# Decode attention with a gated MLP on one core: probabilities written by ScalarE, one accumulator row block, and another order of the last weight loads

## The chip, the cores and the metric

One core of a Trainium2 chip runs the whole program. The metric is the device time of one execution in microseconds (us). The kernel before takes 348.27 us (median of 3 runs, 348.23 to 348.41).

## What is computed

One decode step for two batch rows: attention over a long cache, a small MLP, and a gate that mixes the two.

```python
# x: (2, 1, 512), K and V cache: (2, 32 heads, 4096, 128), all bf16
g = sigmoid((x * gate_w).sum(-1))
q = (x @ wq) as 32 heads of 128          # wq: 512 x 4096
p = softmax(q . k_cache / sqrt(128))     # per batch row and head, over 4096 keys
a = (p . v_cache) as 4096 values @ wo    # wo: 4096 x 512
b = relu(x @ w1) @ w2                    # w1: 512 x 1376, w2: 1376 x 512
out = g * a + (1 - g) * b                # (2, 1, 512)
```

K and V are 134 MB together; the four weight matrices add 11 MB. Every byte is read once.

## The kernel before

**Steps.** The work is cut into `NS` = 16 steps. Step `s` takes four heads (`T` = 4) of one batch row; `quad(s)` gives group `g` of eight heads, batch row `b` and half `i`, so a group is complete after four steps (`SPG` = 4), and there are `NG` = 4 groups. K and V of a step are 4 MB each, laid as 128 partitions: head t has partitions 32t to 32t+31, and each partition has 128 keys (`NC`) of 128 elements. K has two buffers (`kpool`), V two (`vpool`).

**One step.** VectorE multiplies K with the query in two halves (`mult`, L219, in place). TensorE sums blocks of the products with an identity matrix into PSUM (`red`, L225, 16 matmuls of 128x512 a half), and VectorE finishes the sum to one score per key (`scores`, L237). ScalarE takes the exponential and the row sums (`probs`, L243: one instruction of 128x128 into a tile `e`, sums into `partials`). VectorE spreads `e` into a zero-padded tile `PT_sb`, in which the four heads' probabilities stand in four columns beside each other (`expand`, L257, a multiply with a mask `tmask`). TensorE multiplies `PT_sb` with V (`pv`, L278, 32 matmuls of 32 weight columns each, in four column groups). Sums over the partitions of a head come from a small matmul (`sums_mm`, L263), their reciprocal times the gate from VectorE (`sums_inv`). ScalarE empties the result out of PSUM with that scale (`evac`, L289), TensorE picks out each head's own column (`comb`, L304), and every second step VectorE writes the finished head outputs into `OT_sb` (`unpack`, L318 and L322).

**Output.** The product with wo (`wo_mm`) and the MLP's second product (`mlp_o`) both add into one PSUM tile `a_ps`, which stays open for the whole kernel. `accumulate` (L326) makes each product as two matmuls of 256 columns, for the left and the right half of the output, in two separate column groups of the array, so `a_ps` is 34 partitions by 256 columns (rows 0 and 1 the left half, rows 32 and 33 the right). At the end one VectorE copy (L442) takes all 34 partitions to `res`, and two DMAs (L444), one issued by SP and one by ScalarE, write the two halves out.

**Order.** The order on each engine is the order in which the program issues it; no scheduler moves anything. All loads are issued by SP, so they form one queue over the 16 DMA engines. A load waits on SP until its buffer is free: K of step s+2 until `red` of step s has read the buffer, V of step s+1 until `pv` of step s-1 has. On TensorE a step runs `sums_mm(s-1)`, `comb(s-2)`, `red(s)`, `pv(s-1)`. On ScalarE it runs `probs(s)`, `evac(s-1)`.

**Loads of weights.** wq is loaded whole first and its 4 MB buffer is later taken by wo. wo of group 0 is loaded in step 2 and of group 1 in step 6. The other two groups, the last two MB of wo, and the whole of w2 follow the last V (L418 to L424), after V of the last step, which comes in three pieces (half, quarter, quarter). After the loop come the last step's `pv`, `evac`, `comb` and `unpack`, with the products of group 2 put around them, then group 3 and w2.

Of the kernel before, what the change touches and what calls it, by code (L numbers as in the profile page):

```python
# [13 lines left out]
T = 4  # L14
# [3 lines left out]
GH = 8  # L18
WH = 16
PT_SLOTS = 3  # L20
AG = 2


@with_exitstack
def kernel(
# [38 lines left out]
    DR = GH * Dh // P  # L64
    DA = Dh // DR
    CW = P // IG
    AR = CG * (AG - 1) + B
    inv_sqrt_dh = 1.0 / (float(Dh) ** 0.5)
    FF = Dff // P
    FREM = Dff - FF * P  # L70
# [102 lines left out]
    nc.vector.memset(heads, 0.0)  # L173
    for t in range(T):
        nc.vector.memset(heads[t * TP : (t + 1) * TP, t::T], 1.0)
    tmask = consts.tile([P, T], bf16, name="tmask")
    nc.vector.memset(tmask, 0.0)
    for t in range(T):
        nc.vector.memset(tmask[t * TP : (t + 1) * TP, t : t + 1], 1.0)
    PT_sb = consts.tile([P, PT_SLOTS, NQ, CG], bf16, name="PT_sb")  # L180
    nc.vector.memset(PT_sb, 0.0)
    umask = consts.tile([P, DA], fp32, name="umask")
# [3 lines left out]
    partials = consts.tile([P, NS], fp32, name="partials")  # L186
    OT_sb = consts.tile([P, NG, DR, B], bf16, name="OT_sb")
    w2_sb = consts.tile([P, FC, D], bf16, name="w2_sb")
    a_ps = apool.tile([AR, D // AG], fp32, name="a_ps")
    nc.vector.memset(a_ps, 0.0)  # L190
    g_sb = consts.tile([P, B], fp32, name="g_sb")
    omg = consts.tile([P, B], fp32, name="omg")
    hT = consts.tile([P, B, FC], bf16, name="hT")
# [15 lines left out]
            nc.scalar.copy(out=qb[:, b], in_=ps.rearrange("p (i d) -> p i d", d=Dh))  # L209
        qb_t[w] = qb  # L210

    red_t, sc_t, e_t, o_t, osb_t, rsg_t, comb_t = {}, {}, {}, {}, {}, {}, {}

    def mult(s, u):
        g, b, i = quad(s)
        w, gi = divmod(g * IG + i, IW)
        q = qb_t[w][:, b, gi, :].unsqueeze(1).to_broadcast([P, CU, Dh])
        kt = k_t[s][:, u * CU : (u + 1) * CU, :]
        nc.vector.tensor_tensor(out=kt, in0=kt, in1=q, op=ALU.mult)  # L219

    def red(s, u):
        prod = k_t[s][:, u * CU : (u + 1) * CU, :]
        ps = redp.tile([P, CU, RW], fp32, name="red")
        for j in range(Dh // RW):
            nc.tensor.matmul(  # L225
                ps,
                lhsT=ident,
                rhs=prod[:, :, j * RW : (j + 1) * RW],
                start=(j == 0),
                stop=(j == Dh // RW - 1),  # L230
            )
        red_t[s, u] = ps

    def scores(s, u):
        if u == 0:
            sc_t[s] = smalls.tile([P, NC], fp32, name="sc")
        nc.vector.reduce_sum(  # L237
            out=sc_t[s][:, u * CU : (u + 1) * CU], in_=red_t.pop((s, u)), axis=AX.X
        )

    def probs(s):
        e = smalls.tile([P, NC], bf16, name="e")
        nc.scalar.activation(  # L243
            out=e,
            in_=sc_t.pop(s),
            func=ACT.Exp,
            scale=inv_sqrt_dh,
            accum_out=partials[:, s : s + 1],
        )
        e_t[s] = e  # L250

    def expand(s):
        e = e_t.pop(s).rearrange("p (q j) -> p q j", j=JB).unsqueeze(3)
        m = tmask.unsqueeze(1).unsqueeze(1)
        out_ = PT_sb[:, s % PT_SLOTS, :, : JB * T].rearrange("p q (j t) -> p q j t", t=T)
        shape = [P, NQ, JB, T]
        nc.vector.tensor_tensor(  # L257
            out=out_, in0=e.to_broadcast(shape), in1=m.to_broadcast(shape), op=ALU.mult
        )

    def sums_mm(s):
        gs = gsp.tile([P, 1], fp32, name="gs")
        nc.tensor.matmul(gs, lhsT=heads, rhs=partials[:, s : s + 1], start=True, stop=True)  # L263
        rsg_t[s] = gs

    def sums_inv(s):
        rsg = smalls.tile([P, 1], fp32, name="rsg")
        nc.vector.reciprocal(out=rsg, in_=rsg_t[s])
        b = quad(s)[1]
        nc.vector.tensor_tensor(out=rsg, in0=rsg, in1=g_sb[:, b : b + 1], op=ALU.mult)  # L270
        rsg_t[s] = rsg

    def pv(s):
        vt = v_t.pop(s)
        o_ps = opool.tile([P, JB * Dh], fp32, name="o_ps")
        for q in range(NQ):
            k = q % NCG
            nc.tensor.matmul(  # L278
                o_ps[k * CG : (k + 1) * CG, :],
                lhsT=PT_sb[:, s % PT_SLOTS, q, :],  # L280
                rhs=vt[:, q * JB : (q + 1) * JB, :],
                start=(q < NCG),
                stop=(q >= NQ - NCG),
            )
        o_t[s] = o_ps

    def evac(s):
        osb = smalls.tile([P, JB, Dh], fp32, name="osb")
        nc.scalar.activation(  # L289
            out=osb,  # L290
            in_=o_t.pop(s).rearrange("m (j d) -> m j d", d=Dh),
            func=ACT.Copy,
            scale=rsg_t.pop(s),
        )
# [28 lines left out]

    def accumulate(lhsT, rhs, start, stop):
        for k in range(AG):
            nc.tensor.matmul(  # L326
                a_ps[k * CG : k * CG + B, :],
                lhsT=lhsT,
                rhs=rhs[:, k * (D // AG) : (k + 1) * (D // AG)],
                start=start,  # L330
                stop=stop,
            )

    def wo_mm(g, r0=0, r1=DR):
        for r in range(r0, r1):
            accumulate(OT_sb[:, g, r, :], wo_t[g][:, r, :], g == 0 and r == 0, False)

    def gate():
        gwT = transposed(gw_sb, 1, "gwT")
# [31 lines left out]
        if FREM:  # L371
            nc.vector.memset(hT[: P - FREM, :, FF:], 0.0)

    w2_view = B_w2[: FF * P].rearrange("(p f) j -> p f j", f=FF)

    def load_w2(f0, f1):
        nc.sync.dma_start(out=w2_sb[:, f0:f1, :], in_=w2_view[:, f0:f1, :])

    def load_w2_rest():
        nc.sync.dma_start(out=w2_sb[:, FF, :], in_=B_w2[Dff - P :, :])  # L380

    def mlp_o(f0, f1):
        for f in range(f0, f1):
            accumulate(hT[:, :, f], w2_sb[:, f, :], False, f == FC - 1)

    for w in range(NW):
        make_qb(w)
    for s in range(NS):
        if s >= 1:
            sums_mm(s - 1)  # L390
        if s >= 2:
            comb(s - 2)
        mult(s, 0)
        if s == 0:
            gate()
        if s >= 1:
            sums_inv(s - 1)
            expand(s - 1)
        if s >= 2:
            unpack(s - 2)  # L400
        red(s, 0)
        mult(s, 1)
        scores(s, 0)
        red(s, 1)
        scores(s, 1)
        probs(s)
        if s >= 1:
            pv(s - 1)
            evac(s - 1)
        if s % SPG == 1 and SPG < s < NS - SPG:  # L410
            wo_mm(s // SPG - 1)
        if s == 5:
            mlp_h()
        if s % SPG == 2 and s < NS - 2 * SPG:
            load_wo(s // SPG)
        load_k(s + 2)
        load_v(s + 1)
        if s + 1 == NS - 1:  # L418
            load_wo(NG - 2)
            load_wo(NG - 1)  # L420
            load_w2(0, 4)
            load_w2(4, 7)
            load_w2(7, FF)
            load_w2_rest()  # L424

    s = NS - 1
    expand(s)
    sums_mm(s)
    sums_inv(s)
    comb(s - 1)  # L430
    unpack(s - 1)
    pv(s)
    evac(s)
    wo_mm(NG - 2, 0, DR // 2)
    comb(s)
    unpack(s)
    wo_mm(NG - 2, DR // 2, DR)
    wo_mm(NG - 1)
    mlp_o(0, FC)

    res = consts.tile([AR, D // AG], bf16, name="res")
    nc.vector.tensor_copy(out=res, in_=a_ps)  # L442
    for k, queue in enumerate((nc.sync, nc.scalar)):
        queue.dma_start(  # L444
            out=out[:, 0, k * (D // AG) : (k + 1) * (D // AG)],
            in_=res[k * CG : k * CG + B, :],
        )


# [28 lines left out]
```

The softmax here doesn't subtract the row's maximum and nothing guards it: scores larger than these inputs give would overflow.

## Time and profile before

| What | Value |
| --- | --- |
| Median of 3 runs | 348.27 us (348.23 to 348.41) |
| The profiled execution's own time | 348.23 us |
| Its span in the profile | 346.5 us (1.73 us lie around it) |
| Read from HBM | 145.46 MB, 420 GB/s over the span |
| TensorE matmul busy | 214.3 us (62%) |
| VectorE busy | 184.1 us (53%) |
| ScalarE busy | 21.8 us (6%) |
| Mean granted TensorE clock | 0.813 of full speed |

The span runs from the first to the last recorded event of one execution. A row of ten digits or more in the profile shows a busy share in tenths over 40 equal slices of the span, here of 8.66 us each. A row of a group of instructions has the source line, the engine, the operation, the tile written and those read, the shapes and count, then the total busy time and the mean of one in nanoseconds, then the idle time just before them and what ended it. In a timeline, the columns are start in us, duration in us, engine, line, operation and count, and in brackets the idle time before with what ended it. Neighbours of one kind are merged there, and their duration is then that of the batch.

### The profile page before, as it was taken

Reading aid. Unit: us, or ns where it says so; the run is one execution under the profiler, and the core shown is the slowest. Engines: PE = TensorE matmul, PEld = TensorE weight load, DVE = VectorE, ACT = ScalarE, POOL = GpSimd, SP = SyncE. Lnnn points to the kernel's source line nnn. Section 1 sums busy time; section 2 is a strip of 40 time slices with the busy share of each in tenths; the row PEclk is TensorE's granted clock in tenths of the full one; section 3 lists DMA queues with packets and bytes.
Section 4 is the critical chain, followed back from the end, with each engine's and each line's share of the span. In section 5 each row is a group of like instructions: output and inputs, shape, how many; then the busy total and the mean of one; then the engine's idle time right before and its main releaser. Section 6 shows DMA issues by size and latency. Waiting matters only on the chain.

```text
span 346.5 us, 3157 instructions
## 1 busy us (share of the span) xinstructions
PE 214.3 (62%) x1390; PEld 97.5 (28%) x1390; DVE 184.1 (53%) x151; ACT 21.8 (6%) x56; POOL 3.0 (1%) x11
## 2 busy tenths in 40 slices
PE   0437493946719389674918468492929568392965
PEld 0113141322303136231403224131313224131333
DVE  3038665639075482919347291936647291845611
ACT  1020001010100101010100101000010101000020
POOL 3000000000000000000000000000000000000000
PEclk9996787896967879695967859787887859587899
DMA  8999999999999999999999999999999999999993
GB/s 326 446 435 426 404 455 439 435 426 417 428 428 437 435 435 433 428 422 422 437 435 431 437 439 424 428 426 431 428 434 443 431 424 426 431 428 435 410 417 150
DMA packets 6364, 145.67 MB, mean 420 GB/s; under 512 B 711, under 2 KB 846, under 8 KB 1230
## 3 DMA queue, kind: packets, MB, share of 16 engines
q1 hardware_dynamic: 6340, 145.46, 98.0%
q8 instruction: 11, 0.18, 0.2%
q14 instruction: 3, 0.02, 0.0%
q10 hardware_dynamic: 10, 0.00, 0.0%
HBM read 145.46 MB, written 0.00 MB: 420 GB/s over the span
## 4 chain that ended last, share of the span: by engine, by line
DMA 66%; PE 18%; DVE 16%; issue 0%; SPq 0%; DVEq 0%
DMA kt<-in_A_k_cache_dram 51%; PE red L225 17%; DVE kt L219 14%; DMA vt<-in_A_v_cache_dram 10%; DMA w_sb<-in_B_w_dram 5%; PE o_ps L278 1%; DVE PT_sb L257 1%; DVE OT_sb L322 0%; DVE sc L237 0%; DVE tmp L318 0%; PE a_ps L326 0%; DVE rsg L270 0%; DVE gwb L341 0%; DVE res L442 0%; SPq L97 0%
## 5 line engine op out<-in xcount | busy, mean ns | idle before, releaser
L225 PE MATMUL red<-kt,ident 128*128 128x512 bf16 x512 | 147.5, 457 | 96.4 <-DVE kt L219 96.4
L225 PEld LDWEIGHTS <-ident 128*128 128x128 bf16 x512 | 58.2, 114 | 181.4 <-issue 112.6
L219 DVE TENSOR_TENSOR kt<-kt,qb_157 128x8192 bf16<-128x8192 bf16 x16 | 70.7, 4420 | 47.9 <-DMA kt<-in_A_k_cache_dram 47.9
L219 DVE TENSOR_TENSOR kt<-kt,qb_194 128x8192 bf16<-128x8192 bf16 x16 | 70.7, 4421 | 41.7 <-DMA kt<-in_A_k_cache_dram 41.7
L237 DVE TENSOR_REDUCE sc<-red 128x64 f32<-128x512 f32 x32 | 22.1, 691 | 53.6 <-PE red L225 53.6
L278 PE MATMUL o_ps<-vt,PT_sb 128*32 128x512 bf16 x512 | 30.7, 380 | 0.6 <-DMA vt<-in_A_v_cache_dram 0.6
L243 ACT ACTIVATE e<-sc 128x128 bf16<-128x128 f32 x16 | 5.0, 310 | 272.9 <-DVE sc L237 272.9
L304 PE MATMUL comb<-osb,sel 128*64 128x128 f32 x128 | 17.4, 279 | 7.0 <-ACT osb L289 7.0
L278 PEld LDWEIGHTS <-PT_sb 128*32 128x32 bf16 x512 | 12.2, 96 | 17.7 <-issue 7.4
L304 PEld LDWEIGHTS comb<-osb,sel 128*64 128x64 f32 x128 | 13.5, 136 | 8.3 <-ACT osb L289 7.4
L202 PE MATMUL mm<-w,xb 128*32 128x512 bf16 x64 | 6.3, 533 | 12.8 <-DMA w<-in_A_wq_dram 10.7
L289 ACT ACTIVATE osb<-o_ps,rsg 128x512 f32<-128x512 f32 x16 | 11.0, 687 | 14.5 <-PE o_ps L278 14.5
L257 DVE TENSOR_TENSOR PT_sb<-e,tmask 128x512 bf16<-128x512 bf16 x16 | 11.0, 686 | 0.5 <-ACT e L243 0.5
L202 PEld LDWEIGHTS <-xb 128*32 128x32 bf16 x64 | 2.3, 119 | 16.4 <-issue 15.5
L263 PEld LDWEIGHTS gs<-partials,heads 128*128 128x128 f32 x32 | 4.8, 188 | 7.5 <-issue 5.1
L263 PE MATMUL gs<-partials,heads 128*128 128x1 f32 x32 | 6.1, 260 | 1.2 <-ACT e L243 1.2
L318 DVE TENSOR_TENSOR tmp<-comb,umask 128x128 f32<-128x128 f32 x8 | 2.3, 284 | 7.4 <-PE comb L304 7.4
L326 PE MATMUL a_ps<-w,OT_sb 128*2 128x256 bf16 x64 | 4.3, 272 | 2.2 <-DMA w<-in_A_wo_dram 2.2
L345 PE MATMUL mm<-xT,gwb 128*128 128x2 bf16 x4 | 0.3, 170 | 6.2 <-DVE gwb L341 6.2
L326 PEld LDWEIGHTS <-OT_sb 128*2 128x2 bf16 x64 | 2.7, 83 | 4.0 <-issue 2.4
L243 ACT ACTIVATION_READ_ACCUMULATOR e<-sc 128x1 f32 x16 | 3.0, 188 | 0.0
L270 DVE TENSOR_TENSOR rsg<-rsg,g_sb 128x1 f32<-128x1 f32 x16 | 2.5, 159 | 0.6
(40 smaller groups left out, 26.4 us busy)
## 6 DMA issues: line engine op xcount, KB each, us to landing
kt<-in_A_k_cache_dram SPq DMA_DIRECT2D x16, 4096.0 KB, 25.6
vt<-in_A_v_cache_dram SPq DMA_DIRECT2D x15, 4096.0 KB, 33.2
w<-in_A_wq_dram SPq DMA_DIRECT2D x1, 4096.0 KB, 12.3
w<-in_A_wo_dram SPq DMA_DIRECT2D x4, 1024.0 KB, 34.2
vt<-in_A_v_cache_dram SPq DMA_DIRECT2D x1, 2048.0 KB, 17.9
vt<-in_A_v_cache_dram SPq DMA_DIRECT2D x2, 1024.0 KB
w_sb<-in_B_w_dram SPq DMA_DIRECT2D x1, 1376.0 KB
w_sb<-in_B_w_dram SPq DMA_DIRECT2D x2, 384.0 KB, 22.4
```

The costliest lines, as they stand in the source:

```text
L202: nc.tensor.matmul(ps[t * TP : (t + 1) * TP, :], lhsT=xb[:, b, c, :], rhs=wq[:, c, t, :, :], start=(c == 0), stop=(c == DC - 1),)
L219: nc.vector.tensor_tensor(out=kt, in0=kt, in1=q, op=ALU.mult)
L225: nc.tensor.matmul(ps, lhsT=ident, rhs=prod[:, :, j * RW : (j + 1) * RW], start=(j == 0), stop=(j == Dh // RW - 1),)
L237: nc.vector.reduce_sum(out=sc_t[s][:, u * CU : (u + 1) * CU], in_=red_t.pop((s, u)), axis=AX.X)
L243: nc.scalar.activation(out=e, in_=sc_t.pop(s), func=ACT.Exp, scale=inv_sqrt_dh, accum_out=partials[:, s : s + 1],)
L257: nc.vector.tensor_tensor(out=out_, in0=e.to_broadcast(shape), in1=m.to_broadcast(shape), op=ALU.mult)
L263: nc.tensor.matmul(gs, lhsT=heads, rhs=partials[:, s : s + 1], start=True, stop=True)
L270: nc.vector.tensor_tensor(out=rsg, in0=rsg, in1=g_sb[:, b : b + 1], op=ALU.mult)
L278: nc.tensor.matmul(o_ps[k * CG : (k + 1) * CG, :], lhsT=PT_sb[:, s % PT_SLOTS, q, :], rhs=vt[:, q * JB : (q + 1) * JB, :], start=(q < NCG) ...
L289: nc.scalar.activation(out=osb, in_=o_t.pop(s).rearrange("m (j d) -> m j d", d=Dh), func=ACT.Copy, scale=rsg_t.pop(s),)
L304: nc.tensor.matmul(ps[CW * i : CW * (i + 1), :], lhsT=sel[:, j, :], rhs=osb[:, j, :], start=(j == 0), stop=(j == JB - 1),)
L326: nc.tensor.matmul(a_ps[k * CG : k * CG + B, :], lhsT=lhsT, rhs=rhs[:, k * (D // AG) : (k + 1) * (D // AG)], start=start, stop=stop,)
```

## The change

Five things are different in the kernel after:

1. `probs` writes the exponentials straight into `PT_sb`, as four ScalarE instructions of 32 partitions each, one for each head with its own column offset. The tiles `e` and `tmask` and the VectorE step `expand` are gone.
2. `a_ps` is 2 partitions by 512 columns, and each product is one matmul of 512 columns (`accumulate` is gone, and so is the memset of `a_ps`).
3. wo of group 2 is loaded in step 10 instead of behind the last V. Behind the last V now come w2 chunks 0 to 3, wo of group 3, the remainder chunk of w2 (number 10), and w2 chunks 4 to 9 as one DMA.
4. The tail is a part of the loop, which runs to `NS + 2`: the products of a group follow `comb` and `unpack` of its last step, two steps after it; in the last pass w2 chunks 0 to 3 come between `comb` and `unpack`, and the remainder with chunks 4 to 9 ends the program's matmuls.
5. The result is copied in two halves, the left by VectorE and the right by ScalarE, into one tile, and written by one DMA from SP. In the built program ScalarE's copy waits for VectorE's.

```diff
     def probs(s):
-        e = smalls.tile([P, NC], bf16, name="e")
-        nc.scalar.activation(
-            out=e, in_=sc_t.pop(s), func=ACT.Exp, scale=inv_sqrt_dh,
-            accum_out=partials[:, s : s + 1],
-        )
-        e_t[s] = e
-    def expand(s):
...
-        nc.vector.tensor_tensor(
-            out=out_, in0=e.to_broadcast(shape), in1=m.to_broadcast(shape), op=ALU.mult
-        )
+        sc = sc_t.pop(s)
+        for t in range(T):
+            r = slice(t * TP, (t + 1) * TP)
+            nc.scalar.activation(
+                out=PT_sb[r, s % PT_SLOTS, :, t : T * JB : T],
+                in_=sc[r].rearrange("p (q j) -> p q j", j=JB),
+                func=ACT.Exp, scale=inv_sqrt_dh,
+                accum_out=partials[r, s : s + 1],
+            )
...
-    def accumulate(lhsT, rhs, start, stop):
-        for k in range(AG):
-            nc.tensor.matmul(a_ps[k * CG : k * CG + B, :], lhsT=lhsT,
-                rhs=rhs[:, k * (D // AG) : (k + 1) * (D // AG)], start=start, stop=stop)
+    def wo_mm(s):
+        g, b, i = quad(s)
+        if i != IG - 1 or b != B - 1:
+            return
+        for r in range(DR):
+            nc.tensor.matmul(a_ps, lhsT=OT_sb[:, g, r, :], rhs=wo[:, r, :], ...)
...
+    def mlp_o(f0, f1, last):
+        order = list(range(f0, f1))
+        if FREM and f1 == FC:
+            order = [FF] + order[:-1]
+        for f in order:
+            nc.tensor.matmul(a_ps, lhsT=hT[:, :, f], rhs=w2_sb[:, f, :], ...)
...
-    for s in range(NS):
+    for s in range(NS + 2):
...
+        if s == NS + 1:
+            mlp_o(0, 4, False)
...
-            expand(s - 1)
...
-        if s % SPG == 1 and SPG < s < NS - SPG:
-            wo_mm(s // SPG - 1)
+        if s >= 2:
+            wo_mm(s - 2)
...
-        if s % SPG == 2 and s < NS - 2 * SPG:
+        if s % SPG == 2 and s < NS - SPG:
             load_wo(s // SPG)
...
         if s + 1 == NS - 1:
-            load_wo(NG - 2)
-            load_wo(NG - 1)
             load_w2(0, 4)
-            load_w2(4, 7)
-            load_w2(7, FF)
-            load_w2_rest()
+            load_wo(NG - 1)
+            load_w2(4, FC)       # the remainder chunk first, then chunks 4 to 9
+    mlp_o(4, FC, True)
...
-    res = consts.tile([AR, D // AG], bf16, name="res")
-    nc.vector.tensor_copy(out=res, in_=a_ps)
-    for k, queue in enumerate((nc.sync, nc.scalar)):
-        queue.dma_start(...)
+    res = consts.tile([B, D], bf16, name="res")
+    nc.vector.tensor_copy(out=res[:, : D // 2], in_=a_ps[:, : D // 2])
+    nc.scalar.copy(out=res[:, D // 2 :], in_=a_ps[:, D // 2 :])
+    nc.sync.dma_start(out=out[:, 0, :], in_=res)
```

More of the change, by code (lines that the diff above doesn't have):

```diff
@@ L20 @@
 PT_SLOTS = 3
-AG = 2
 @with_exitstack
@@ L66 @@
     CW = P // IG
-    AR = CG * (AG - 1) + B
     inv_sqrt_dh = 1.0 / (float(Dh) ** 0.5)
@@ L175 @@
         nc.vector.memset(heads[t * TP : (t + 1) * TP, t::T], 1.0)
[L176 to L179, printed above, removed]
     PT_sb = consts.tile([P, PT_SLOTS, NQ, CG], bf16, name="PT_sb")
@@ L188 @@
     w2_sb = consts.tile([P, FC, D], bf16, name="w2_sb")
-    a_ps = apool.tile([AR, D // AG], fp32, name="a_ps")
-    nc.vector.memset(a_ps, 0.0)
+    a_ps = apool.tile([B, D], fp32, name="a_ps")
     g_sb = consts.tile([P, B], fp32, name="g_sb")
@@ L210, in make_qb @@
         qb_t[w] = qb
-    red_t, sc_t, e_t, o_t, osb_t, rsg_t, comb_t = {}, {}, {}, {}, {}, {}, {}
+    red_t, sc_t, o_t, osb_t, rsg_t, comb_t = {}, {}, {}, {}, {}, {}
     def mult(s, u):
@@ L241, in probs @@
     def probs(s):
-        e = smalls.tile([P, NC], bf16, name="e")
[L243 to L247, printed above, removed]
-            accum_out=partials[:, s : s + 1],
-        )
-        e_t[s] = e
-    def expand(s):
[L253 to L257, printed above, removed]
-            out=out_, in0=e.to_broadcast(shape), in1=m.to_broadcast(shape), op=ALU.mult
-        )
+        sc = sc_t.pop(s)
[4 more added lines that the diff above has]
+                in_=sc[r].rearrange("p (q j) -> p q j", j=JB),
+                func=ACT.Exp,
+                scale=inv_sqrt_dh,
+                accum_out=partials[r, s : s + 1],
+            )
     def sums_mm(s):
@@ L322, in unpack @@
             nc.vector.reduce_sum(out=OT_sb[:, g, :, b], in_=tmp, axis=AX.X)
-    def accumulate(lhsT, rhs, start, stop):
-        for k in range(AG):
[L326 to L331, printed above, removed]
-            )
-    def wo_mm(g, r0=0, r1=DR):
-        for r in range(r0, r1):
-            accumulate(OT_sb[:, g, r, :], wo_t[g][:, r, :], g == 0 and r == 0, False)
+    def wo_mm(s):
+        g, b, i = quad(s)
+        if i != IG - 1 or b != B - 1:
+            return
+        wo = wo_t[g]
+        for r in range(DR):
+            nc.tensor.matmul(
+                a_ps,
+                lhsT=OT_sb[:, g, r, :],
+                rhs=wo[:, r, :],
+                start=(g == 0 and r == 0),
+                stop=False,
+            )
     def gate():
@@ L372, in mlp_h @@
             nc.vector.memset(hT[: P - FREM, :, FF:], 0.0)
-    w2_view = B_w2[: FF * P].rearrange("(p f) j -> p f j", f=FF)
     def load_w2(f0, f1):
[L377 to L384, printed above, removed]
+        if f1 == FC and FREM:
+            nc.sync.dma_start(out=w2_sb[:, FF, :], in_=B_w2[Dff - P :, :])
+            f1 = FF
+        view = B_w2[: FF * P].rearrange("(p f) j -> p f j", f=FF)
+        nc.sync.dma_start(out=w2_sb[:, f0:f1, :], in_=view[:, f0:f1, :])
+    def mlp_o(f0, f1, last):
[3 more added lines that the diff above has]
+        for f in order:
+            nc.tensor.matmul(
+                a_ps,
+                lhsT=hT[:, :, f],
+                rhs=w2_sb[:, f, :],
+                start=False,
+                stop=(last and f == order[-1]),
+            )
     for w in range(NW):
         make_qb(w)
-    for s in range(NS):
-        if s >= 1:
+    for s in range(NS + 2):
+        if 1 <= s <= NS:
             sums_mm(s - 1)
@@ L392 @@
             comb(s - 2)
-        mult(s, 0)
+        if s == NS + 1:
+            mlp_o(0, 4, False)
+        if s < NS:
+            mult(s, 0)
         if s == 0:
             gate()
-        if s >= 1:
+        if 1 <= s <= NS:
             sums_inv(s - 1)
-            expand(s - 1)
         if s >= 2:
             unpack(s - 2)
[L401 to L407, printed above, removed]
+        if s < NS:
+            red(s, 0)
+            mult(s, 1)
+            scores(s, 0)
+            red(s, 1)
+            scores(s, 1)
+            probs(s)
+        if 1 <= s <= NS:
             pv(s - 1)
             evac(s - 1)
-        if s % SPG == 1 and SPG < s < NS - SPG:
-            wo_mm(s // SPG - 1)
+        if s >= 2:
+            wo_mm(s - 2)
         if s == 5:
             mlp_h()
-        if s % SPG == 2 and s < NS - 2 * SPG:
+        if s % SPG == 2 and s < NS - SPG:
             load_wo(s // SPG)
@@ L418 @@
         if s + 1 == NS - 1:
-            load_wo(NG - 2)
+            load_w2(0, 4)
             load_wo(NG - 1)
-            load_w2(0, 4)
-            load_w2(4, 7)
-            load_w2(7, FF)
-            load_w2_rest()
[L426 to L439, printed above, removed]
-    res = consts.tile([AR, D // AG], bf16, name="res")
-    nc.vector.tensor_copy(out=res, in_=a_ps)
-    for k, queue in enumerate((nc.sync, nc.scalar)):
[L444 to L447, printed above, removed]
+            load_w2(4, FC)
[4 more added lines that the diff above has]
+    nc.sync.dma_start(out=out[:, 0, :], in_=res)
 _INS = ['A_x', 'A_k_cache', 'A_v_cache', 'A_wq', 'A_wo', 'B_x', 'B_w1', 'B_w2', 'gate_w']
```

## The prediction, made before the result was known

> **What bounds the kernel now.** I read the slices first, then the DMA queues, the waits, and the timeline of the last 17 us.
>
> ```profile
> DMA  8999999999999999999999999999999999999993
> ...
> q1 hardware_dynamic: 6340, 145.46, 98.0%
> q8 instruction: 11, 0.18, 0.2%
> ```
>
> The sixteen DMA engines are at 90% or more from the second slice to the last but one, and SP's loads (q1) fill 98.0% of their time. The whole list of waits says the same from the other side:
>
> ```profile
> DVE kt L219 <- DMA kt<-in_A_k_cache_dram: 89.5, 15, 16.1
> ```
>
> VectorE stands still 89.5 us in 15 waits for K, 6.0 us a step. So the span is a stream of bytes plus what follows its last byte, and only three things can move it: bytes, the stream's pace, and the work behind the last landing. Two stretches of the windows view and the timeline show that end (windows: start:end, length, then PE, PEld, DVE, ACT, POOL busy, granted clock, DMA share, GB/s):
>
> ```profile
> 330.00:340.00 10.00, 6.67 (x90) 3.75 (x79) 1.60 (x5) 1.78 (x4) 0.00 (x0) 1.00 1.00 410
> 340.00:343.30 3.30, 2.19 (x32) 1.36 (x33) 0.00 (x0) 0.00 (x0) 0.00 (x0) 1.00 0.36 132
> ```
>
> ```profile
> 335.03 0.61 PE L278 MATMUL o_ps<-vt,PT_sb 128*32 128x512 bf16 x8 [0.58 <-DMA vt<-in_A_v_cache_dram]
> ...
> 335.74 0.69 ACT L289 ACTIVATE osb<-o_ps,rsg 128x512 f32<-128x512 f32 x1 [3.84 <-PE o_ps L278]
> 337.51 0.60 PE L326 MATMUL a_ps<-w,OT_sb 128*2 128x256 bf16 x8 [1.87 <-DMA w<-in_A_wo_dram]
> ...
> 340.00 1.04 PE L326 MATMUL a_ps<-w,OT_sb 128*2 128x256 bf16 x16 [0.34 <-DMA w<-in_A_wo_dram]
> ...
> 343.25 0.60 PE L326 MATMUL a_ps<-w_sb,hT 128*2 128x256 bf16 x8 [0.52 <-DMA w_sb<-in_B_w_dram]
> 343.25 0.39 PEld L326 LDWEIGHTS <-hT 128*2 128x2 bf16 x7 [0.71 <-issue]
> 343.89 0.42 DVE L442 CAST res<-a_ps 34x256 bf16<-34x256 f32 x1 [4.11 <-PE a_ps L326]
> 344.34 0.33 SPq L444 DMA_DIRECT2D out_dram<-res  x1
> 344.34 0.26 ACTq L444 DMA_DIRECT2D out_dram<-res  x1
> ```
>
> See how each batch of output products waits for its own landing: wo of group 2 at 337.51, of group 3 at 340.00, the last two pieces of w2 at 343.25. The remainder was issued at 330.04 and landed 13.5 us later (its source view), at 343.52. After that come 0.35 us of matmuls (to 343.87), 0.42 us of copy, and 2.16 us from the DMA issue to the end. The clock is at full speed here.
>
> **What the Trainium skill says.** "TensorE: Matmul & The Clock Gate", Back-to-back issue gap and Single matmul latency: a warm matmul of 512 columns follows the one before after about 216 ns, and one alone takes (398+N)/2.4 ns, so 272 ns at 256 columns and 379 at 512. The trace agrees: 272 ns mean in the row of L326, 380 in the row of `pv`. "PSUM — Partial Sum Buffer", PSUM bank collisions: two engines must not touch the same bank in the same 32-partition quadrant, even at different columns. In the old `a_ps` the two halves lie in two quadrants; in the new one both copies read one quadrant, which is why ScalarE's copy waits for VectorE's. No run here shows a collision. "ScalarE: Activation LUTs", What ACT_TABLE_LOAD costs: an instruction with immediate scale and bias takes 186 + 0.833 N ns, so 399 ns at N = 256 (estimate). The nearest row, the copy of L209 at N = 512, has 586 ns against 612 by that formula, so 0.39 us is used. "Runtime: NRT & Kernel Launch", Instruction fetch mechanics: engines fetch instructions in 16 KiB blocks of 256 over a DMA queue. The queue q8 above shows 11 of them with 0.18 MB; at 0.2% of 16 engines' span each takes about 1.0 us of one engine.
>
> **The change part by part.**
>
> *Exponentials on ScalarE.* Two rows carry it:
>
> ```profile
> L243 ACT ACTIVATE e<-sc 128x128 bf16<-128x128 f32 x16 | 5.0, 310 | 272.9 <-DVE sc L237 272.9
> ...
> L257 DVE TENSOR_TENSOR PT_sb<-e,tmask 128x512 bf16<-128x512 bf16 x16 | 11.0, 686 | 0.5 <-ACT e L243 0.5
> ...
> L243 ACT ACTIVATION_READ_ACCUMULATOR e<-sc 128x1 f32 x16 | 3.0, 188 | 0.0
> ```
>
> VectorE loses 16 x 0.686 = 11.0 us. ScalarE goes from one to four pairs a step, each still of 128 elements a partition: 4 x (0.31 + 0.19) = 2.0 us, or 1.6 with the 0.1 us overlap that the timeline shows in a pair (311.02 and 311.23). That is 1.1 to 1.5 us later for two waiters. `sums_mm(s)` heads the next step on TensorE, with `comb` (1.09 us) and `red` queued behind it; but `red` waits for `mult`, 4.42 us after K, and K is some 6 us late. `evac(s-1)` stands behind `probs(s)` on ScalarE, and its reader `comb` comes a step later. Neither K's release (`red`) nor V's (`pv(s-1)`, which uses probabilities a step old) waits on ScalarE. Value taken: 0 on the path, hidden by the K wait. Bounds: 0 below, as the stream never waits for VectorE, and +0.3 above for the last step, where the cover is short.
>
> *wo of group 2 in step 10.* One issue of 0.43 us on SP, ahead of K of step 12, V of step 11 behind it; SP waits for buffers up to 30 us a time, so 0. K and V after it land later by the 1 MB it takes, 2.49 us (340.00 - 337.51 for the next megabyte), and the tail carries one megabyte less: the sum of bytes is the same. Its 8 matmuls run in step 13, under the K wait, at 8 x 0.216 = 1.7 us: 0. The w2 rows of 6 KB in place of two of 3 KB save some 0.05 us by the packets in the trace (3 KB takes 124 ns, 8 KB 312). Last landing: 343.52 - 0.05 = 343.47. The order of the DMAs behind the last V, four in place of six, costs SP nothing.
>
> *Does the tail keep up?* V's last piece moves from 334.98 to 337.47. Eight `pv` matmuls to 338.12, `evac` to 338.91, `comb` (1.09) to 340.04, four w2 products to 340.9, `unpack` to 340.7. wo of group 3 lands at 341.23 (337.47 + 1.27 for 512 KB + 2.49), its eight matmuls keep TensorE until 343.0, the remainder until 343.2. The last DMA lands at 343.47, 0.3 us later. So the landing still sets the end, by little. The last `pv` begins near 335.7, since `comb(14)` stands ahead of it and waits for `evac(14)` behind the four exponentials; its first three quarters need 1.5 us, to 337.2, again 0.3 us ahead of V's last piece.
>
> *Behind the last landing.* Before, the last two matmuls ran side by side in two column groups. Now six of 512 columns follow each other, as chunks 4 to 9 come in one DMA: 343.51 + 5 x 0.216 + 0.38 = 344.97, **+1.10** against 343.87. VectorE's copy is again 256 columns wide: 0.42, to 345.41 (0.27 to 0.42 as a bound, the 2-partition shape is not in the trace). Then **+0.49**: 0.10 us from VectorE to ScalarE (310.92 to 311.02 at the scores) and 0.39 for the copy, to 345.90 (bound 0.27 to 0.6). The DMA is issued at 345.93 in place of 344.34; one DMA with rows of 1 KB instead of two with 512 B changes its 2.16 us by less than 0.05 either way.
>
> Sum: 345.93 - 344.34 = 1.59, so a span of 348.1 and 348.23 + 1.59 = 349.82. The profiled execution is 0.04 under the median, so against the median 349.86; I say **349.8 us**, rounded down for the small savings. The memsets of `a_ps` and `tmask` at the start lie under the wq load: 0.
>
> **The rivals.**
>
> *The slowest DMA engines are less late (not slower).* In 340.00 to 343.30 the mean engine works 0.36 x 3.3 = 1.2 us, so it is through near 341.2, while the last packet ends at 343.04: two engines carry about 1.8 us more than the mean. Instruction fetches of some 1.0 us on single engines make such lags, and the change shortens TensorE's program by 86 instructions. If the fetches fall elsewhere, everything in the tail comes up to 1.8 us earlier: 349.8 - 1.8 = 348.0. It decides from 0.85 us on, where 348.97, the edge of no change, is reached; both late engines must gain one fetch. One fetch gives 348.8. Against it: nearly the same program is fetched in the same order. Chance 0.11.
>
> *The tail becomes longer.* The same fetches add one to a late engine, +1.0 to 1.2, 351.0; or the margins of 0.3 us in the tail fail by half a microsecond, 350.3. Chance 0.12.
>
> *ScalarE's chain slows the stream.* 1.5 us a step on 16 steps would be +24 us, 373, if the K waits were no cover; they are, with 6 us a step. Chance 0.02.
>
> *VectorE's 11 us are worth something.* If VectorE were the bound, 349.8 - 11 = 339. The 89.5 us of K waits speak against it. Chance 0.02.
>
> **How the numbers follow.** The forecast has 0.73 and its own range, from the bounds of the copies and the tail, is 349.4 to 350.3. Slower or faster counts from 0.2% (0.7 us), about what a measurement of this kernel can tell: under 347.57 or over 348.97. Slower: 0.73 + 0.12 + 0.02, less 0.02 of the forecast's chance that I put below the edge, makes 0.85. No change: those 0.02 and 0.09 of the first rival, 0.11. Faster: the first rival's other 0.02, if it takes the full 1.8 us or the copies come cheap as well, and VectorE's 0.02, 0.04. The range reaches to both shifts of one fetch, 348.5 to 351.0.
>
> **What would show it.** Right: ScalarE's busy time near 46 us and VectorE's near 173, the DMA slices unchanged; a last batch of six `a_ps` matmuls of about 1.46 us that begins near 343.5; a VectorE copy near 345.0, ScalarE's near 345.5, the output's issue near 345.9. Wrong: a last landing off 343.5 by over 0.8 us (the DMA engines' lag moved), a gap between slices (the stream starved), or last matmuls that follow each other without a wait for the last w2 (the tail was the bound).

## The result, and the profile after

The kernel after takes **349.86 us** (median of 4 runs, 349.83 to 349.94) beside 348.34 for the kernel before in the same comparison. The ratio is 1.0043, 95% interval 1.0026 to 1.0061. The change makes the kernel 0.4% slower, 1.5 us. The profiled execution took 349.83 us with a span of 348.1.

From the page of the kernel after, the DMA slices and the queues, and from its whole list of waits the one line that answers to the wait for K:

```profile
DMA  8999999999999999999999999999999999999991
...
q1 hardware_dynamic: 6196, 145.46, 97.6%
q8 instruction: 10, 0.16, 0.2%
```

```profile
DVE kt L212 <- DMA kt<-in_A_k_cache_dram: 97.3, 15, 16.9
```

The stream is as full as it was: 90% or more from the second slice to the last but one, for the same bytes. VectorE lost 9.8 us of busy time and waits 7.8 us longer for K. Only the last slice has moved, from 3 tenths to 1: the DMA engines are idle for a larger part of the end. The timeline of that end, in the kernel after:

```profile
336.33 1.95 PE L263 MATMUL o_ps<-vt,PT_sb 128*32 128x512 bf16 x32
338.37 0.69 ACT L274 ACTIVATE osb<-o_ps,rsg 128x512 f32<-128x512 f32 x1 [3.11 <-PE o_ps L263]
...
341.40 1.89 PE L315 MATMUL a_ps<-w,OT_sb 128*2 128x512 bf16 x8 [0.25 <-DMA w<-in_A_wo_dram]
...
343.13 1.91 PE L371 MATMUL a_ps<-w_sb,hT 128*2 128x512 bf16 x7
343.58 0.95 PEld L371 LDWEIGHTS <-hT 128*2 128x2 bf16 x5 [0.37 <-issue]
345.07 0.41 DVE L421 CAST res<-a_ps 2x256 bf16<-2x256 f32 x1 [4.22 <-PE a_ps L371]
345.52 0.36 ACT L422 CAST res<-a_ps 2x256 bf16<-2x256 f32 x1 [6.46 <-DVE res L421]
345.91 0.33 SPq L423 DMA_DIRECT2D out_dram<-res  x1
```

The matmul line at 343.13 hides a wait, because neighbours are merged: its first matmul, the remainder chunk, runs at 343.13, the other six from 343.58, where the weight load below it goes on. The last DMA was issued at 318.0 and landed 25.5 us later, at 343.54. So the landing sets the start of the last six matmuls, at nearly the same time as the last landing in the kernel before (343.52). From the landing to the end of the last matmul are 1.50 us (to 345.04), where before had 0.33 (to 343.85), then 0.87 us to the output's issue in place of 0.49. From the issue to the end are 2.19 us, 2.16 before.

The groups of the four exponentials have a surprise, to which I come back:

```profile
L238 ACT ACTIVATE PT_sb<-sc 32x128 bf16<-32x128 f32 x64 | 30.5, 477 | 262.5 <-DVE sc L230 261.7
...
L238 ACT ACTIVATION_READ_ACCUMULATOR PT_sb<-sc 32x1 f32 x64 | 15.5, 243 | 0.0
```

### The profile page after: what moved, and what is told of

The parts are those of the page before. It is cut to its first block, busy times and chain, and to the rows that moved or that the text cites. A ratio compares the mean times of both kernels' runs of the same rounds, so it can differ in the third digit from the quotient of the medians.

```text
span 348.1 us, 3131 instructions
## 1 busy us (share of the span) xinstructions
PE 216.4 (62%) x1347; PEld 96.8 (28%) x1347; DVE 174.3 (50%) x129; ACT 46.2 (13%) x153; POOL 3.0 (1%) x11
## 4 chain that ended last, share of the span: by engine, by line
DMA 66%; PE 22%; DVE 11%; issue 0%; SPq 0%; ACT 0%; DVEq 0%
DMA kt<-in_A_k_cache_dram 59%; PE red L218 21%; DVE kt L212 10%; DMA w_sb<-in_B_w_dram 7%; PE a_ps L371 0%; DVE sc L230 0%; DVE gwb L326 0%; DVE res L421 0%; SPq L95 0%; ACT res L422 0%; PE mm L330 0%; DVE gwT L161 0%; DVEq L212 0%
## 5 line engine op out<-in xcount | busy, mean ns | idle before, releaser
L218 PE MATMUL red<-kt,ident 128*128 128x512 bf16 x512 | 145.4, 454 | 87.4 <-DVE kt L212 87.4
L238 ACT ACTIVATE PT_sb<-sc 32x128 bf16<-32x128 f32 x64 | 30.5, 477 | 262.5 <-DVE sc L230 261.7
L238 ACT ACTIVATION_READ_ACCUMULATOR PT_sb<-sc 32x1 f32 x64 | 15.5, 243 | 0.0
L195 PE MATMUL mm<-w,xb 128*32 128x512 bf16 x64 | 5.4, 471 | 12.7 <-DMA w<-in_A_wq_dram 10.7
L315 PE MATMUL a_ps<-w,OT_sb 128*2 128x512 bf16 x32 | 7.6, 379 | 0.2 <-DMA w<-in_A_wo_dram 0.2
L253 DVE RECIPROCAL rsg<-gs 128x1 f32<-128x1 f32 x16 | 2.6, 161 | 2.5 <-PE gs L248 2.5
L202 ACT CAST qb_150<-mm 128x512 bf16<-128x512 f32 x2 | 1.2, 586 | 13.7 <-PE mm L195 13.7
## 6 DMA issues: line engine op xcount, KB each, us to landing
w_sb<-in_B_w_dram SPq DMA_DIRECT2D x1, 768.0 KB, 25.5
```

The lines of the kernel that those rows point to most:

```text
L195: nc.tensor.matmul(ps[t * TP : (t + 1) * TP, :], lhsT=xb[:, b, c, :], rhs=wq[:, c, t, :, :], start=(c == 0), stop=(c == DC - 1),)
L218: nc.tensor.matmul(ps, lhsT=ident, rhs=prod[:, :, j * RW : (j + 1) * RW], start=(j == 0), stop=(j == Dh // RW - 1),)
L238: nc.scalar.activation(out=PT_sb[r, s % PT_SLOTS, :, t : T * JB : T], in_=sc[r].rearrange("p (q j) -> p q j", j=JB), func=ACT.Exp, scale=i ...
L315: nc.tensor.matmul(a_ps, lhsT=OT_sb[:, g, r, :], rhs=wo[:, r, :], start=(g == 0 and r == 0), stop=False,)
```

## The experiments

The theory: the last landing did not move, and the loss is what stands behind it (six wide matmuls from one DMA, and two copies in a row). The rivals: the exponentials on ScalarE, or the new order of loads, delay the stream; or the row of wide matmuls, not the landing, sets the end. Medians of before in these comparisons lie between 348.38 and 348.50.

### The exponentials alone (e1_exps_alone)

```diff
 # on the kernel before
-        nc.scalar.activation(out=e, in_=sc_t.pop(s), ...)          # and expand(s)
+        for t in range(T):                                         # as in after
+            nc.scalar.activation(out=PT_sb[r, slot, :, t : T * JB : T], in_=sc[r], ...)
```

> The kernel before with one part of the change alone: the four ScalarE exponentials per step that write PT_sb, and no VectorE spreading step. Theory (the landing of the last weights sets the end, and ScalarE's longer chain lies under the wait for K): 348.3 us, no change within 0.2 us; ScalarE busy near 46 us; the last landing still near 343.5. Rival 'VectorE's 11 us are worth something': 337 to 346. Rival 'ScalarE's chain slows the stream': 350 or more, with a last landing after 345.

Measured: 348.34 us (13 runs), ratio 0.9996, interval 0.9988 to 1.0004. VectorE's busy time fell from 184.1 to 174.5 us and ScalarE's rose to 45.8, and nothing came of it. Its list of waits shows where VectorE's time went, to K:

```profile
DVE kt L215 <- DMA kt<-in_A_k_cache_dram: 93.1, 15, 16.6
```

That is 93.1 us in place of 89.5. In the tail ScalarE's last `evac` does begin 0.7 us later (336.44 against 335.74), but TensorE's next products wait for wo of group 2 in both kernels (until 337.67 and 337.51), which hides it. Both rivals on this step fall.

### The accumulator alone (e2_accumulator_alone)

```diff
 # on the kernel before
-AG = 2
+AG = 1          # a_ps 2x512; the copies and the one output DMA of after
```

> The kernel before with the other arithmetic part alone: one accumulator of 2x512, one matmul of 512 columns for each product, the two copies one after the other, one output DMA; the loads stay as they were. Theory: the last piece of w2 is small here, so three matmuls follow the landing at 343.21 and one the landing at 343.52: the last matmul ends near 344.28 in place of 343.87 (+0.41), the output is issued near 345.2 in place of 344.34, in all +0.9 us: 349.2. Rival 'the two copies are the whole loss and the width of the matmuls costs nothing': +0.5, 348.8. Rival 'the load order is the whole loss': 348.3.

Measured: 349.61 us (7 runs), ratio 1.0043, interval 1.0027 to 1.0060; 0.4 above what I expected. The runs lie in two groups, four from 349.08 to 349.61 and three from 350.78 to 350.97. The trace is of the lower group; what makes the upper one is not shown. The timeline and the waits of its last 9 us tell why the lower one is above 349.2:

```profile
339.76 2.75 PE L325 MATMUL a_ps<-w,OT_sb 128*2 128x512 bf16 x12
...
342.35 2.54 PE L325 MATMUL a_ps<-w_sb,hT 128*2 128x512 bf16 x11
```

```profile
PE a_ps L325 <- DMA w<-in_A_wo_dram: 1.9, 1, 1.9
```

Twenty-three matmuls of 512 columns follow each other from 339.76 to 344.89 without a wait, 0.216 us apart, and the list has no wait for w2 at all, only the one for wo of group 2. In this order of loads the wide matmuls make TensorE the bound of the last 5 us. My 344.28 assumed that the landing set the end. That is the rival of the tail that becomes longer, in another place than where I had looked for it.

### The halves put back (e3_two_halves)

```diff
 # on the kernel after
-            nc.tensor.matmul(a_ps, lhsT=..., rhs=...)              # 512 columns
+            accumulate(...)                                       # two of 256, as in before
+    nc.vector.tensor_copy(out=res, in_=a_ps)                       # and two output DMAs
```

> The kernel after with the accumulator of before put back: each product as two matmuls of 256 columns in two column groups, one VectorE copy, two output DMAs. Exponentials, loads and order stay those of after. Theory: six pairs follow the last landing (343.54) instead of six matmuls of 512: 343.58 + 5 x 0.107 + 0.272 = 344.39 against 345.04, and the copies cost 0.42 instead of 0.84: output issued near 344.86, in all -1.05 us: 348.8. It stays 0.5 above before, since the last DMA carries six chunks. Rival 'the load order or the exponentials moved the last landing': it stays near 349.8. Rival 'the accumulator is the whole loss': 348.3.

Measured: 348.89 us (13 runs), ratio 1.0013, interval 1.0005 to 1.0021, where 348.8 was expected. Of the 1.5 us, 1.0 is gone.

```profile
343.61 0.82 PE L314 MATMUL a_ps<-w_sb,hT 128*2 128x256 bf16 x12 [0.99 <-DMA w_sb<-in_B_w_dram]
344.47 0.41 DVE L422 CAST res<-a_ps 34x256 bf16<-34x256 f32 x1 [3.57 <-PE a_ps L314]
```

The same six chunks now take 0.82 us behind the landing, in pairs, against 1.46; TensorE waits 0.99 us for them. The landing itself is at 343.57 by the trace. The loads and the exponentials of after are all in this kernel, so they did not move it.

### Small last pieces (e4_small_last)

```diff
 # on the kernel after
-            load_w2(4, FC)         # remainder, then chunks 4 to 9 in one DMA
+            load_w2(4, 7)
+            load_w2(7, FF)
+            nc.sync.dma_start(out=w2_sb[:, FF, :], in_=B_w2[Dff - P :, :])
```

> The kernel after with the last w2 in three DMAs, chunks 4 to 6, 7 to 9 and then the remainder, so that little follows the last landing; the 512-column matmuls and the copies stay. Theory: the landing stops being the bound and the row of matmuls behind wo of group 3 becomes it: eight and seven matmuls of 512 columns from 341.40 end at 341.40 + 14 x 0.216 + 0.38 = 344.80 in place of 345.04, so only -0.25 us: 349.6, and no wait for w2 is left. Rival 'six matmuls in one DMA are the cost of 1.1 us': -0.75, 349.1.

Measured: 349.48 us (7 runs), ratio 1.0028, interval 1.0018 to 1.0039: 0.4 below after, where the row of wide matmuls had been worked out to leave 0.25 and the rival 0.75. From its timeline:

```profile
341.37 1.89 PE L315 MATMUL a_ps<-w,OT_sb 128*2 128x512 bf16 x8 [0.16 <-DMA w<-in_A_wo_dram]
343.09 1.67 PE L366 MATMUL a_ps<-w_sb,hT 128*2 128x512 bf16 x7
```

Seven matmuls take 1.67 us, six steps of 0.216 and one of 0.38, so none of them waits; they end at 344.76. With wide matmuls the row behind wo of group 3 can't end sooner, and in after the landing was only 0.2 us later than that row.

### Both together (e6_halves_and_small_last)

The edits of e3_two_halves and e4_small_last in one kernel.

> The kernel after with both: the accumulator, copy and output DMAs of before, and the last w2 in three DMAs with the remainder at the end. The exponentials on ScalarE, wo of group 2 in step 10 and the order of the tail stay those of after. Theory: what follows the last landing (near 343.55) is again one pair of matmuls, one copy and the output, so it ends as before did: 348.4 us, within 0.2 of before. Rival 'moving wo of group 2 forward costs something of its own': over 348.7.

Measured: 348.31 us (13 runs), ratio 1.0000, interval 0.9992 to 1.0008. Its last batch of products:

```profile
343.10 0.60 PE L314 MATMUL a_ps<-w_sb,hT 128*2 128x256 bf16 x8 [0.51 <-DMA w_sb<-in_B_w_dram]
```

It is the batch of before (343.25, 0.60 us). All of the loss is gone, though the exponentials, wo of group 2 in step 10 and the tail's order are still those of after. Neither of the two is enough alone: the halves give 1.0, the small pieces 0.4 with wide matmuls and 0.6 with halves.

### One copy in place of two (e7_one_copy)

```diff
 # on the kernel after
-    nc.vector.tensor_copy(out=res[:, : D // 2], in_=a_ps[:, : D // 2])
-    nc.scalar.copy(out=res[:, D // 2 :], in_=a_ps[:, D // 2 :])
+    nc.vector.tensor_copy(out=res, in_=a_ps)
```

> The kernel after with VectorE copying all 512 columns of the result, no ScalarE copy. Theory: a copy of 256 columns takes 0.41 us, and 256 more columns [...](the scores reduce 512 columns in 0.69) make it 0.69; it takes the place of 0.41 + 0.04 + 0.36 + 0.03 = 0.84, so -0.15 us: 349.7. If the two copies had run beside each other in after, one wide copy would be slower by 0.25: 350.1.

Measured: 349.78 us (5 runs), ratio to before 1.0042, interval 1.0029 to 1.0054. Its last copy and the issue:

```profile
345.06 0.68 DVE L421 CAST res<-a_ps 2x512 bf16<-2x512 f32 x1 [4.25 <-PE a_ps L371]
345.77 0.33 SPq L422 DMA_DIRECT2D out_dram<-res  x1
```

The one wide copy takes 0.68 us and the issue comes 0.71 after its start, 0.84 in after. The median is 0.08 lower, too little for the runs to settle alone; the timeline shows the gain of 0.13. Cutting the copy over two engines was worth less than nothing here, as the second waited for the first.

### More instructions (e8_more_instructions)

```diff
 # on the kernel before
             comb(s - 2)
+            spare(64)      # 64 matmuls of 128x2 into a PSUM tile that nothing reads
         mult(s, 0)
```

> The kernel before with 64 extra small matmuls (128x2, nothing reads them) in each step from the third on, put where TensorE waits for K: 1792 more TensorE instructions, seven more blocks of 16 KB on the instruction queue. Theory (each fetch holds one DMA engine for about 1.1 us, and the end waits for the slowest engine): the mean engine is 7 x 1.1 / 16 = 0.5 us later; the slowest, by where the fetches fall, 0 to 2.4 later, most likely one fetch, 1.2: 349.5 us, with a last landing near 344.7. If fetches cost the stream nothing: 348.4 and a landing at 343.5. If the extra matmuls themselves were on the path: 4 us a step, 400.

Measured: 350.26 us (4 runs: 349.69, 349.75, 350.77, 350.93), ratio 1.0059, interval 1.0044 to 1.0075; 0.8 above the value expected, within the 0 to 2.4. The median falls between two clumps 1.1 us apart; the trace is of the run of 349.75, and the upper clump has none. From its page, and its timeline:

```profile
q8 instruction: 18, 0.29, 0.3%
```

```profile
344.76 0.61 PE L326 MATMUL a_ps<-w_sb,hT 128*2 128x256 bf16 x8 [0.28 <-DMA w_sb<-in_B_w_dram]
345.41 0.41 DVE L450 CAST res<-a_ps 34x256 bf16<-34x256 f32 x1 [2.79 <-PE a_ps L326]
```

Eighteen blocks in place of eleven, as 1792 / 256 = 7 says. TensorE has a lower clock here (0.61 from 340.0 to 343.3, where before has 1.00), but it still waits for w2, so the landings set the end. The completion marks of the last DMA, one for each DMA engine, are in the trace: the first engine is through at 340.20 (340.26 before), the median at 342.46 (341.73), the last at 345.06 (343.52). The earliest engine is where it was, so the stream as a whole was not held up, and the slowest is 1.54 us later. More fetches made the late engines later: this is the mechanism of the rival of the DMA engines, in the direction that costs time. Which engine a fetch holds is not recorded.

### The exponentials, written contiguously (e9_exps_contiguous)

```diff
 # on the kernel before
+        for t in range(T):
+            nc.scalar.activation(out=e[r], in_=sc[r], ...)         # VectorE spreads e as before
```

> The kernel before with the exponential as four instructions of 32 partitions that write the contiguous tile e; VectorE spreads it as before. A look at one duration: after has 477 ns for an exponential of 32 partitions that writes every fourth element of PT_sb, where before has 310 ns for 128 partitions written contiguously. If the spread write is the cause, it is 310 ns here; if it is the cut into four or the partition offset, 477. The time stays 348.4 in either case.

Measured: 348.43 us in one run. Its group:

```profile
L246 ACT ACTIVATE e<-sc 32x128 bf16<-32x128 f32 x64 | 19.6, 307 | 265.5 <-DVE sc L237 264.9
```

307 ns, as for 128 partitions. So neither the cut into four nor the partitions made it slower; the write to every fourth element did, from 307 to 477 ns. The reading of the sum went from 184 to 243 with it.

### Fewer instructions, and a kernel faster than both

If fetches make the slowest DMA engine late, fewer instructions should help. The next four kernels build on e6_halves_and_small_last. In them VectorE adds the two halves of each key's products ahead of `red` (the fold), which rounds the sum of two products to bf16 once more than before; e13_fold_bf16_pick also rounds the partial sums that `comb` adds.

```diff
 # e10: a fold ahead of red, which then has 8 matmuls a half
+    def fold(s, u):
+        kt = ...                                               # half u of step s's products
+        nc.vector.tensor_tensor(out=kt[:, :, :64], in0=kt[:, :, :64], in1=kt[:, :, 64:], op=ALU.add)
 # e11: not in the last step; e12: not in the last three
 # e13: e11 with osb and sel in bf16
```

> The counter-test to the run with more instructions, and an attempt at a kernel faster than both. On the kernel with the halves of before and the small last pieces (e6_halves_and_small_last), VectorE adds the two halves of each key's 128 products (64 + 64) before the reduction, so TensorE needs 16 matmuls a step for it in place of 32: 512 instructions fewer, two blocks of 16 KB less to fetch. VectorE has 2 x 2.2 us more a step (half of a multiply's 4.42), some 16 us of a step's 20, still under the wait for K. Theory (the end waits for the DMA engine that the most fetches have held): nine fetches in place of eleven, the mean engine 0.13 us earlier, the slowest 0 to 1.2 earlier: 347.1 to 348.3 us, the last landing between 342.3 and 343.4. If fetches are not what makes the slowest engine late: 348.3 and 343.4. If VectorE became the bound: over 350.

Measured: 349.71 us (16 runs, 349.06 to 350.35), ratio 1.0034, interval 1.0027 to 1.0042: slower, and outside all three cases as I had put them. From its page, and its timeline:

```profile
q8 instruction: 9, 0.15, 0.2%
```

```profile
316.80 4.43 DVE L215 TENSOR_TENSOR kt<-kt,qb 128x8192 bf16<-128x8192 bf16 x1 [1.58 <-DMA kt<-in_A_k_cache_dram]
...
334.05 2.24 PE L271 MATMUL o_ps<-vt,PT_sb 128*32 128x512 bf16 x32
...
343.18 1.04 PE L319 MATMUL a_ps<-w,OT_sb 128*2 128x256 bf16 x16 [0.17 <-DVE OT_sb L315]
344.05 0.93 PE L319 MATMUL a_ps<-w_sb,hT 128*2 128x256 bf16 x14
```

The landing did come earlier: the last completion mark is at 342.40, against 343.37 in e6_halves_and_small_last. (Eight fetches had begun by then, against eleven there; the ninth began at 344.68, behind the landing.) But the step of the last K now takes 17.3 us from its multiply to the product with V behind it, 13.7 in before, and the products wait for VectorE (`OT_sb`) instead of for a landing. The cover that the wait for K gives ends with the last K.

> e10_fewer_instructions with the fold left out of the last step alone. There the last landing had come 1.1 us earlier (342.40 against 343.52 in before), but VectorE and TensorE were late behind the last K (17.3 us from its multiply to the last-but-one product with V, 13.7 in before), so the end was set by TensorE at 345.0. Theory: with the last step as short as in before, the landing sets the end again, and the gain of the fetches shows: last matmuls near 342.8, output issued near 343.2, 347.2 us, 0.3% faster than before. If the last step is not what was late, or the fetches fall on other engines once more: 348.3 or over.

Measured: 348.30 us (14 runs), ratio 0.9994, interval 0.9986 to 1.0002, where the theory had 347.2. Two runs had 347.21 and 347.42, the others 348.09 to 348.87. The profiled one, of 348.87 us and the slowest of them, shows the other case:

```profile
343.47 1.02 PE L322 MATMUL a_ps<-w_sb,hT 128*2 128x256 bf16 x8 [2.04 <-DMA w_sb<-in_B_w_dram]
```

TensorE waits 2.04 us for w2, and then takes 1.02 us for the eight matmuls that take 0.60 in before, so some 0.4 us of this run is TensorE's own. By the completion marks of the last DMA fifteen engines were through at 342.19 and one at 343.63. Two DMAs earlier all sixteen had been through by 340.90; the ninth fetch began at 341.22, and it fits in place and size as what held the one engine.

> The same with the fold left out of the last three steps, so that VectorE has caught up before the last K whatever the TensorE clock. TensorE's program is 64 instructions longer, still nine or ten blocks. Theory: 347.2 us as well if the fetches fall as in e10_fewer_instructions, and a narrower spread of the runs than 349.06 to 350.35; up to 348.4 if a fetch falls on a late engine.

Measured: 348.31 us (13 runs, 348.03 to 348.99), ratio 0.9999, interval 0.9991 to 1.0007, again above the 347.2.

```profile
343.23 0.60 PE L322 MATMUL a_ps<-w_sb,hT 128*2 128x256 bf16 x8 [0.51 <-DMA w_sb<-in_B_w_dram]
```

Fifteen engines through at 342.33, one at 343.49; the ninth fetch began at 337.4. Ending the fold earlier changed nothing, and TensorE's last batch waits for w2 here as well, until 343.23: the late engine sets the end.

> e11_fold_but_last with the step's result copied out of PSUM in bf16 instead of fp32, and the selecting matrix of comb in bf16 (the partial sums of a head are rounded to bf16 before they are added). TensorE then runs comb in 4 pairs a step in place of 8, 128 instructions fewer: the ninth block of instructions, whose fetch at 341.2 held one DMA engine for 1.5 us just before the last landing in e11_fold_but_last, is not reached. Theory: the first eight fetches leave all engines within about 0.8 us of each other there (landings of V's and w2's pieces), so the last landing is near 342.3 and the time 347.2 us, the value that two of that kernel's fourteen runs had (347.21 and 347.42). If which engine a fetch holds is chance from run to run, the runs lie between 347.1 and 348.5 in clumps about 1.1 us apart.

Measured: **347.76 us** (16 runs, 346.89 to 347.96), ratio 0.9980, interval 0.9972 to 0.9987: faster than both kernels, and above the 347.2 expected. From the page, the timeline and the windows view of its end:

```profile
q8 instruction: 8, 0.13, 0.2%
```

```profile
339.93 1.87 PE L322 MATMUL a_ps<-w,OT_sb 128*2 128x256 bf16 x16 [1.33 <-DMA w<-in_A_wo_dram]
341.59 1.71 PE L322 MATMUL a_ps<-w_sb,hT 128*2 128x256 bf16 x14
```

```profile
338.00:343.50 5.50, 3.96 (x39) 2.10 (x38) 0.75 (x3) 0.00 (x0) 0.00 (x0) 0.53 0.50 195
```

Eight fetches; the last mark is at 342.15 and all sixteen are within 2.1 us. Over all the traces, the last mark of the loads stands at 342.15 and 342.40 where eight fetches had begun before it, at 343.49 and 343.63 with nine, between 343.37 and 343.79 with ten or eleven, and at 345.06 with eighteen. So fewer is earlier, but not step by step: nine land no earlier than ten or eleven. The rest that I had hoped for went to TensorE: in these 5.5 us it has 0.53 of its clock, and the sixteen matmuls of wo of group 3 take 1.87 us where the kernel before has 1.04. Behind the landing of wo at 339.93 its row is the bound now, not the last landing.

## Why the prediction was right

The forecast was 349.8 us in a range of 348.5 to 351.0, with slower at 0.85. It came out at 349.86, and by the steps it was built of:

- **The landing stays.** Forecast 343.47, measured 343.54. Moving a megabyte of wo ahead of V and 1 MB less behind it cancelled, as e3_two_halves (343.57, with all of after's loads) and e6_halves_and_small_last (343.37, with wo moved as in after) show. The prediction took the last landing alone as the limit of before. Two limits meet there: the row of pairs that the landing before it released at 343.25 comes to its fourth pair at 343.57, with or without the remainder's landing at 343.52.
- **Six wide matmuls behind it.** Forecast +1.10 us to 344.97, measured +1.19 to 345.04, 1.46 us from the first to the end as worked out from 0.216 and 0.38. The end of before's row was read as 343.87; by its line it is 343.85. The section of the Trainium skill that the 216 ns are from ("TensorE: Matmul & The Clock Gate", Back-to-back issue gap) also gives about 131 ns a matmul for a long stream of weight loads and matmuls, which the prediction did not weigh. The runs decide for 0.216: e2_accumulator_alone has 23 in a row at that distance.
- **Two copies in a row.** Forecast 0.42 + 0.10 + 0.39, measured 0.41 + 0.04 + 0.36: the hand-over to ScalarE was sized at 0.10 from the scores and took 0.04. The issue was forecast at 345.93 and came at 345.91. The later landing and the quicker copies hid each other, so that last agreement is in part luck. Why ScalarE's copy waits was not tried: the shared quadrant that the prediction names is one candidate, the tile `res` that both copies write is another.
- **Exponentials at nothing.** Right for the path (e1_exps_alone), wrong in two sizes. The step took each at 310 ns; it is 477, so the four take 1.95 us (332.59 to 334.54) and ScalarE is 1.5 us later, the top of the bound. Its busy time of 46.2 agreed with the forecast by luck: the forecast had the exponential too short, and left the overlap of a pair in the sum, and the two cancelled.
- **Does the tail keep up.** Right by less than I said. The last product with V was to begin near 335.7 and wait for V's last piece; it began at 336.33 and ran through without a wait on record, and its `evac` was at 338.37, 0.15 later than forecast. The margin of 0.3 us there was gone; the one behind wo of group 3 was 0.2 and held. e2_accumulator_alone and e4_small_last show the row of wide matmuls as the bound as soon as the order of loads leaves it no gap. I gave that rival the chance of failing by its margins alone and did not see that it was already the second limit everywhere.
- **The rival of the DMA engines.** Not in after: ten fetches, and the same landing. But that the number of fetches moves the last landing is shown in both directions, by e8_more_instructions and by e13_fold_bf16_pick beside e11_fold_but_last. That it depends on which engine a fetch holds is argued from the one late engine of e11_fold_but_last; that this differs between runs of one kernel is argued from the clumps of its times, and its faster runs have no trace. Neither is shown.

The Trainium skill ("Runtime: NRT & Kernel Launch", Instruction fetch mechanics) gives 256 instructions to a block and calls the cost of crossing a boundary mostly hidden. The counts agree: 1792 instructions more gave seven blocks more, 512 fewer gave two fewer. For the engine that executes them it may be hidden; for a stream that ends with its slowest DMA engine it was not, 1.54 us for seven blocks.

## What to carry to other kernels

In a kernel that a full stream of loads bounds, look for the last landing and cost only what stands behind it: how much of the last DMA's work can't begin before it, whether that work runs side by side or in a row, and how many hand-overs lie between it and the output. Make the last DMA small, but first check that the engine behind it has a gap left; if its row is the bound, a smaller DMA buys little. Work moved off an engine that waits for the stream was worth nothing here (e1_exps_alone); work added to it cost nothing that shows until the stream's last buffer, where it was suddenly on the path (e10_fewer_instructions).

## What the runs showed of the hardware that I had not expected

- A ScalarE exponential of 128 elements a partition takes 477 ns when it writes every fourth bf16 element and 307 when it writes them side by side; 32 partitions cost what 128 do.
- Each block of instructions came as one DMA packet of 16 KB that took about 1.1 us (1.00 to 1.13 in before), while the loads ran. In e11_fold_but_last one engine ended 1.4 us behind the other fifteen after such a fetch. The first and the last engine ended 3.3 us apart in before (340.26 and 343.52), and the program waits for the last; how much of that the fetches make is not shown.
- With less TensorE work the clock granted was lower, not higher: 0.72 in e10_fewer_instructions, where TensorE is busy 53% of the span, against 0.793 and 62% in e6_halves_and_small_last. A single reduction matmul of 512 columns took 613 ns in the mean there against 457. What made the clock fall was not tried.
